# Keys first: another load and work order, running KV sums, and one kind of PSUM tile, in a gated mix of linear attention and an MLP

## The chip, the cores and the metric

The kernel runs on one core of a Trainium2 chip. The metric is the device time of a run in microseconds (us), the median of several runs. The "span" of a profile is shorter, because it goes from the core's first to its last instruction: for the kernel before, 165.8 us of span stand for about 167.5 us of time. Engines: PE is TensorE's matmuls, PEld its weight loads, DVE is VectorE, ACT is ScalarE, POOL is GpSimd, SP is SyncE, which here only issues transfers (SPq).

## The reference, cut to what matters

x is 2048 tokens by 448, in bf16. Branch A is linear attention with 16 heads of 28 and softmax features; branch B is an MLP with tanh gelu, 448 to 1792 and back. A gate g per token mixes them.

```python
q, k, v = split(x @ wqkv)                       # 16 heads of 28
phi_q = concat([softmax(q @ w_phi), softmax(-(q @ w_phi))])
phi_k = concat([softmax(k @ w_phi), softmax(-(k @ w_phi))])
kv, z = phi_k.T @ v, phi_k.sum(0)               # sums over all 2048 tokens
a = ((phi_q @ kv) / (phi_q @ z + 1e-6)) @ wo
b = gelu(x @ w1 + b1) @ w2 + b2
g = sigmoid((x * gate_w).sum(-1))
out = g * a + (1 - g) * b
```

The projection weights are folded with w_phi on the chip (Wpk for keys, Wpq for queries) before any key or query can be computed; keys need an exponential on ScalarE, then sums and reciprocals on VectorE, then a normalisation; all key tiles have to be summed into kv before the first "nm" tile (numerator and denominator); and PE does the rest.

## The kernel before: the parts that the change and the argument touch

The main order, with what each step is called in the profile in the comments:

```python
for t in range(4):
    v_tile(t, late=True)         # v: 4 matmuls of 448 columns into a one-bank PSUM tile
prep(WkT, Wpk)                   # w_ps: fold w_phi into the key weights, copies by DVE and ACT
prep_twice(WqT, Wpq)             # w_ps: the same for queries
k_pair(0)
k_pair(1)
late_logits(range(4))            # l_ps: the gate logits of the first four tiles
for u in range(2, 4):
    v_tile(2 * u); v_tile(2 * u + 1); k_pair(u)
b1_turn()                        # b1p: transpose the MLP's bias b1
for u in range(4, 8):
    v_tile(2 * u); v_tile(2 * u + 1); k_pair(u); q_pair(u - 4, 0)
q_pair(0, 1); q_pair(1, 1)
kv_group(0)                      # 32 matmuls of 116 columns over all key tiles
q_pair(2, 1); kv_group(1); q_pair(3, 1); kv_group(2); kv_group(3)
# [...]  gate, gelu table
for t in range(2): num_tile(t)   # nm, then a chain of 11 DVE instructions, then a transposing DMA to oT
for n in range(28): m_unit(n // 14, n % 14)      # hp: 14 row-paired matmuls, then gelu on ACT
for t in range(16):
    if t + 2 < 16: num_tile(t + 2)
    # y: 4 matmuls of oT with wo, 14 of gel with w2, then scaled on ACT (res) and stored
```

```python
def k_pair(u):
    pk = pair("pk")              # a two-bank PSUM tile
    # [...] 8 matmuls of 448 columns
    nc.scalar.activation(out=phik[:, tt, 0, :], in_=pk[:, :, 0:D], func=ACT.Exp)
    nc.scalar.activation(out=phik[:, tt, 1, :], in_=pk[:, :, 0:D], func=ACT.Exp, scale=-1.0)
    nc.vector.reduce_sum(out=sums[:], in_=ph, axis=AX.X)
    nc.vector.reciprocal(out=rec[:], in_=sums[:])
    eng = nc.vector if u >= 6 else nc.gpsimd
    eng.tensor_tensor(out=ph, in0=ph, in1=rec[...], op=ALU.mult)
```

PSUM has four one-bank tiles (v, w_ps, kv, nm) and two two-bank tiles (pk, pq, hp, y), so nm never takes a buffer from hp or y.

The softmax here doesn't subtract the row's maximum and nothing guards it: scores larger than these inputs give would overflow.

## Time and profile before

| | before |
|---|---|
| time | 167.38 us median (3 runs) |
| span | 165.8 us |
| PE busy | 159.1 us, 96% |
| PE's waits after the warm-up | 1.7 us in five places, the longest 0.5 |
| DVE, ACT busy | 84.3 and 79.6 us |
| clock granted to PE in every slice | 1.00 |

How to read it: an engine that is busy 96% of the span, and whose few waits are all short, sets the span. The lines that carry this reading are in the prediction below.

### The profile page before, as it was taken

To read this page: it belongs to the slowest core of one execution; us is meant where nothing else is said; L and a number is where in the kernel's file an instruction comes from. 1 tells how busy PE (TensorE), PEld (TensorE's weight loads), DVE (VectorE), ACT (ScalarE), POOL (GpSimd) and SP (SyncE) were. 2 spreads that over 40 slices of the span, in tenths; PEclk is the share of its full clock that TensorE was granted. 3 is DMA by queue.
4 is the path that set the end of the run, shared out by engine and by line. 5 is a ranking of instruction groups with operands and counts; after the bars stand their busy time and mean duration, and the time that the engine had idled before them with its cause. 6 is when DMAs were issued, how large, how long until landed. Compare 5 with 4: busy or idle time off the path is not lost.

```text
span 165.8 us, 3129 instructions
## 1 busy us (share of the span) xinstructions
PE 159.1 (96%) x1278; PEld 84.6 (51%) x1278; DVE 84.3 (51%) x250; ACT 79.6 (48%) x99; POOL 25.6 (15%) x36
## 2 busy tenths in 40 slices
PE   6899999999999999999999999999999999999991
PEld 2356544444366855444545445555555555555450
DVE  1255699975981286000000004887877777778300
ACT  2045877889884477777777775111112211111111
POOL 5810099996000000000000000000000000000000
PEclk9999999999999999999999999999999999999999
DMA  5999989999900001100000000222222253325300
GB/s 118 224 214 152 215 169 227 214 209 232 338 9 4 4 2 32 36 0 0 0 4 0 0 4 0 59 59 63 60 59 61 59 65 76 72 60 63 89 28 28
DMA packets 28348, 13.72 MB, mean 83 GB/s; under 512 B 21805, under 2 KB 27438, under 8 KB 28334
## 3 DMA queue, kind: packets, MB, share of 16 engines
q1 hardware_dynamic: 27310, 13.09, 37.5%
q10 hardware_dynamic: 960, 0.43, 1.2%
q8 instruction: 10, 0.16, 0.4%
q14 instruction: 4, 0.03, 0.1%
q0 software_dynamic: 64, 0.00, 0.0%
HBM read 5.65 MB, written 1.84 MB: 45 GB/s over the span
## 4 chain that ended last, share of the span: by engine, by line
PE 73%; SPq 10%; DMA 7%; DVE 6%; ACT 1%; issue 1%; DVEq 0%; ACTq 0%
PE hp L336 26%; PE y L394 24%; PE y L391 7%; PE nm L348 4%; PE pq L265 4%; PE kv L278 3%; PE v_ps L184 3%; SPq L115 3%; PE pk L247 3%; DMA xT<-in_A_x_dram 3%; SPq L116 3%; DMA oT<-o_tok 3%; SPq L119 3%; DVE phik L258 2%; DVE sums L254 2%; DMA b1c<-in_B_b_dram 1%
## 5 line engine op out<-in xcount | busy, mean ns | idle before, releaser
L394 PE MATMUL y<-w_sb,gel 128*128 128x448 bf16 x224 | 45.0, 352 | 0.0
L336 PE MATMUL hp<-xT,w_sb 64*128 64x512 bf16 x196 | 42.5, 376 | 0.0
L336 PE MATMUL hp<-xS,w_sb 64*128 64x512 bf16 x196 | 42.5, 376 | 0.0
L339 ACT ACTIVATE gel<-hp,b1T 128x1024 bf16<-128x1024 f32 x28 | 31.2, 1114 | 11.1 <-PE hp L336 10.6
L397 ACT ACTIVATE res<-y,ungate 128x448 bf16<-128x448 f32 x16 | 10.1, 634 | 50.5 <-PE y L394 50.5
L394 PEld LDWEIGHTS <-gel 128*128 128x128 bf16 x224 | 21.9, 98 | 20.5
L336 PEld LDWEIGHTS <-w_sb 64*128 64x128 bf16 x392 | 20.8, 94 | 21.3
L352 DVE COPY st<-nm 128x32 f32<-128x32 f32 x32 | 4.5, 183 | 44.6 <-PE nm L348 44.6
L258 POOL TENSOR_TENSOR phik<-phik,rec 128x1792 bf16<-128x1792 bf16 x6 | 19.1, 3209 | 12.3 <-DVE rec L256 12.3
L254 DVE TENSOR_REDUCE sums<-phik 128x64 f32<-128x1792 bf16 x8 | 16.1, 2007 | 5.5 <-ACT phik L251 5.5
L369 DVE TENSOR_TENSOR tmp<-nm,al 128x448 bf16<-128x448 f32 x32 | 18.4, 615 | 0.0
L391 PE MATMUL y<-wo_sb,oT 128*128 128x448 bf16 x64 | 14.8, 352 | 0.4 <-DMA oT<-o_tok 0.4
L184 PE MATMUL v_ps<-WvG,xT 128*128 128x449 bf16 (+1 forms) x64 | 13.7, 356 | 0.5 <-DMA xT<-in_A_x_dram 0.5
L265 PE MATMUL pq<-xT,Wpq 64*128 64x512 bf16 x56 | 13.5, 377 | 0.3 <-ACT phik L251 0.2
L265 PE MATMUL pq<-xS,Wpq 64*128 64x512 bf16 x56 | 13.4, 377 | 0.0
L247 PE MATMUL pk<-Wpk,xT 128*128 128x448 bf16 x64 | 13.2, 352 | 0.0
L250 ACT ACTIVATE phik<-pk 128x896 bf16<-128x896 f32 x8 | 7.3, 918 | 6.9 <-PE pk L247 6.9
L270 ACT ACTIVATE EqP<-pq 112x1024 bf16<-112x1024 f32 x8 | 8.2, 1024 | 3.2 <-PE pq L265 3.2
L184 PEld LDWEIGHTS <-xT 128*128 128x128 bf16 x64 | 5.8, 99 | 7.5 <-issue 1.5
L247 PEld LDWEIGHTS <-xT 128*128 128x128 bf16 x64 | 6.2, 98 | 5.8
L265 PEld LDWEIGHTS <-Wpq 64*128 64x128 bf16 x112 | 5.1, 94 | 7.4 <-issue 2.4
L348 PE MATMUL nm<-KVbd,EqP 112*128 112x120 bf16 x64 | 8.6, 216 | 0.0
(71 smaller groups left out, 138.0 us busy)
## 6 DMA issues: line engine op xcount, KB each, us to landing
w_sb<-in_B_w_dram SPq DMA_DIRECT2D x3, 1568.0 KB, 18.7
out_dram<-res SPq DMA_DIRECT2D x16, 112.0 KB, 1.9
xS<-xT SPq DMA_DIRECT2D x2, 256.0 KB, 3.8
xS<-xT SPq DMA_DIRECT2D x2, 192.0 KB, 3.6
WvG<-in_A_wqkv_dram ACTq DMA_DIRECT2D x1, 336.0 KB, 3.4
wo_sb<-in_A_wo_dram SPq DMA_DIRECT2D x1, 336.0 KB, 18.7
oT<-o_tok SPq DMA_TRANSPOSE x16, 2.4
xT<-in_A_x_dram SPq DMA_TRANSPOSE x8, 4.5
```

The source lines that it names most:

```text
L184: nc.tensor.matmul(v_ps[:, 0:n], lhsT=xT[:, c, t * P:(t + 1) * P], rhs=WvG[:, c, 0:n], start=(c == 0), stop=(c == NC4 - 1))
L247: nc.tensor.matmul(pk[:, i, 0:D], lhsT=xT[:, c, t * P:(t + 1) * P], rhs=Wpk[:, c, :], start=(c == 0), stop=(c == NC4 - 1))
L254: nc.vector.reduce_sum(out=sums[:], in_=ph, axis=AX.X)
L258: eng.tensor_tensor(out=ph, in0=ph, in1=rec[:, :, None].to_broadcast([P, 64, DH]), op=ALU.mult)
L265: nc.tensor.matmul(pq[:, i, :], lhsT=Wpq[i * HP:(i + 1) * HP, k, g * GW:g * GW + P], rhs=x_half(i, k, h), start=(k == 0), stop=(k == NK - 1))
L336: nc.tensor.matmul(hp[:, i, :], lhsT=w1_sb[i * HP:(i + 1) * HP, k, j * P:(j + 1) * P], rhs=x_half(i, k, h), start=(k == 0), stop=(k == NK ...
L339: nc.scalar.activation(out=gel[:, j, h * 1024:(h + 1) * 1024], in_=hp[:].rearrange("p a b -> p (a b)"), func=ACT.Gelu_apprx_tanh, bias=b1T ...
L348: nc.tensor.matmul(nm[s][:, g * KW:(g + 1) * KW], lhsT=E[0:GW, g, tok], rhs=KVbd[0:GW, g, s, :], start=True, stop=True)
L369: nc.vector.tensor_tensor(out=tmp[:, s, :].rearrange("p (g j d) -> p g j d", g=NG, j=4), in0=nm[s][:, 0:NG * KW].rearrange("p (g c) -> p g ...
L391: nc.tensor.matmul(y, lhsT=oT[:, c, tok], rhs=wo_sb[:, c, :], start=(c == 0), stop=False)
L394: nc.tensor.matmul(y, lhsT=gel[:, j, tok], rhs=w2_sb[:, j, :], start=False, stop=(j == NJ - 1))
L397: nc.scalar.activation(out=res[:], in_=y, func=ACT.Copy, scale=ungate[:, t:t + 1])
```

## The change

Its intent: load and compute the keys first, so that their exponentials, sums and normalisation are under way early; sum kv while keys are still coming, in two PSUM banks that stay open; save PE work by pairing the half-filled last chunk (448 = 3 x 128 + 64) of v with that of k on the two row halves of the array; use two-bank PSUM tiles alone, three of them beside the two open banks, so that v is copied out two tiles at a time; split the gelu buffer, so that the first half can be written while keys are still being summed.

The diff, cut to its core:

```diff
-    ps = ctx.enter_context(tc.tile_pool(name="ps", bufs=4, space=PSUM))   # "one" x4, "pair" x2
+    def pair(name):
+        return ps.tile([P, 2, 512], F32, name=name, tag="pair", bufs=3)
+    acc = ps.tile([P, 2, 512], F32, name="acc", tag="acc", bufs=1)
-    load_x(0); load_wT(WkT, D); load_wT(WqT, 0); load_x(1); load_x(2) [...]
+    load_wT(WkT, D); load_x(0); load_x(1); load_wT(WqT, 0); swap_x(0) [... v weights, load_x(2), ...]
     # order of the work
-    v_tile(0..3); prep(WkT, Wpk); prep_twice(WqT, Wpq); k_pair(0); k_pair(1); late_logits(range(4))
-    [...]
+    dummies(10)
+    prep(WkT, Wpk)
+    dummies(3)
+    for u in range(4):
+        k_pair(u)
+    prep_twice(WqT, Wpq)
+    for u in range(4):
+        q_pair(u, 0)
+        v_pair(u)
+    b1_turn()
+    kv_pair(4); q_pair(0, 1); kv_sum(0); kv_sum(1)
+    kv_pair(5); q_pair(1, 1); kv_sum(2); kv_sum(3)
+    kv_pair(6); q_pair(2, 1); kv_sum(4); kv_pair(7); q_pair(3, 1); kv_sum(5)
     # prep_twice: copies two chunks at a time, on DVE for m = 0 and 2, on ACT for m = 1 and 3
+            copy(m + 1, W_out[:, 2 * m:2 * m + n, 0:D], w_ps[:, 0:n, 0:D])
+    def kv_pair(u):                       # v and k of two token tiles
+        [... c = 0..2 of v, then of k, for both tiles ...]
+        for i in range(2):
+            nc.tensor.matmul(v_ps[:, i, 0:D + 1], lhsT=x3, rhs=WvL[:], start=False, stop=True)
+            nc.tensor.matmul(pk[:, i, 0:D], lhsT=xT[HP:P, 3, ...], rhs=Wpk[HP:P, 3, :], ...)
+        k_out(u, pk)                      # exponentials, sums, reciprocal, normalisation
+        v_out(u, v_ps)                    # copies on DVE
     # hp and y
-    AHEAD = 2
+    AHEAD = 3
+        if n == 2: kv_sum(6); kv_sum(7); kv_out()
+        if n == 4: num_tile(0); num_tile(1)
+    num_tile(2)
```

More of the change, by code (lines that the diff above doesn't have):

```diff
@@ L55 @@
     work = ctx.enter_context(tc.tile_pool(name="work", bufs=2))
-    ps = ctx.enter_context(tc.tile_pool(name="ps", bufs=4, space=PSUM))
-    def one(name):
-        return ps.tile([P, 512], F32, name=name, tag="one", bufs=4)
+    ps = ctx.enter_context(tc.tile_pool(name="ps", bufs=3, space=PSUM))
     def pair(name):
-        return ps.tile([P, 2, 512], F32, name=name, tag="pair", bufs=2)
+        return ps.tile([P, 2, 512], F32, name=name, tag="pair", bufs=3)
     xT = consts.tile([P, NC4, S], BF16, name="xT")
     xS = consts.tile([P, NC4, 2, 512], BF16, name="xS")
+    x3o = consts.tile([HP, 512], BF16, name="x3o")
     w1_sb = consts.tile([P, NK, F], BF16, name="w1_sb")
@@ L82 @@
     ungate = consts.tile([P, NT], F32, name="ungate")
+    hold = ctx.enter_context(tc.tile_pool(name="hold", bufs=1))
+    phik_all = hold.tile([P, NT * 2 * D + 16], BF16, name="phik", tag="phik_gel")
+    phik = phik_all[:, 0:NT * 2 * D].rearrange("p (t s f) -> p t s f", t=NT, s=2)
+    vaug = hold.tile([P, NT, NG, GW + 4], BF16, name="vaug")
     atn = ExitStack()
@@ L86 @@
     WvG = attn.tile([P, NC4, D + 1], BF16, name="WvG")
+    WvL = attn.tile([HP, D + 1], BF16, name="WvL")
     Wpk = attn.tile([P, NC4, D], BF16, name="Wpk")
@@ L93 @@
     bd = attn.tile([P, NC4, H, DH], BF16, name="bd")
-    phik_all = attn.tile([P, NT * 2 * D + 16], BF16, name="phik")
-    phik = phik_all[:, 0:NT * 2 * D].rearrange("p (t s f) -> p t s f", t=NT, s=2)
-    vaug = attn.tile([P, NT, NG, GW + 4], BF16, name="vaug")
     warm = attn.tile([P, 512], BF16, name="warm")
     nc.vector.memset(warm[:], 0.0)
+    nc.vector.memset(wphi[64:P, 3, :], 0.0)
     nc.vector.memset(WvG[0:64, 3, :], 0.0)
-    nc.vector.memset(wphi[64:P, 3, :], 0.0)
-    nc.scalar.dma_start(WvG[:, 0:3, 0:D],
-                        A_wqkv[0:384, 2 * D:3 * D].rearrange("(c p) n -> p c n", p=P))
-    nc.scalar.dma_start(WvG[64:P, 3, 0:D], A_wqkv[384:448, 2 * D:3 * D])
     wphi_rows = A_w_phi.rearrange("h a b -> (h a) b")
@@ L111 @@
     nc.gpsimd.dma_start(WvG[64:P, 3, D:D + 1], gate_w[384:448, None])
+    nc.gpsimd.dma_start(WvL[:, D:D + 1], gate_w[384:448, None])
     def load_x(b):
@@ L119, in load_wT, with swap_x @@
         nc.sync.dma_start_transpose(W[:], A_wqkv[:, base:base + NC4 * P])
-    load_x(0)
-    load_wT(WkT, D)
-    load_wT(WqT, 0)
-    load_x(1)
-    load_x(2)
-    for h in range(2):
-        if h == 1:
-            load_x(3)
+    def swap_x(h):
         ev = slice(2 * h * 512, 2 * h * 512 + 512)
@@ L132 @@
         nc.sync.dma_start(xS[HP:P, 0:3, h, :], xT[0:HP, 0:3, od])
+    load_wT(WkT, D)
+    load_x(0)
+    load_x(1)
+    load_wT(WqT, 0)
+    swap_x(0)
+    nc.sync.dma_start(WvG[:, 0:3, 0:D],
+                      A_wqkv[0:384, 2 * D:3 * D].rearrange("(c p) n -> p c n", p=P))
+    nc.sync.dma_start(WvG[64:P, 3, 0:D], A_wqkv[384:448, 2 * D:3 * D])
+    nc.sync.dma_start(WvL[:, 0:D], A_wqkv[384:448, 2 * D:3 * D])
+    load_x(2)
+    load_x(3)
+    swap_x(1)
+    nc.sync.dma_start(x3o[:], xT[HP:P, 3, 1536:2048])
     nc.sync.dma_start(b1c[:], B_b1.rearrange("(j p) -> j p", p=P))
@@ L177 @@
     nc.gpsimd.memset(o_tok[:, :, D + 1:512], 0.0)
-    def v_tile(t, late=False):
-        v_ps = one("v_ps")
-        n = D if late else D + 1
-        for c in range(NC4):
-            nc.tensor.matmul(v_ps[:, 0:n], lhsT=xT[:, c, t * P:(t + 1) * P],
-                             rhs=WvG[:, c, 0:n], start=(c == 0), stop=(c == NC4 - 1))
-        src = v_ps[:, 0:D].rearrange("p (g d) -> p g d", g=NG)
-        if t % 2 == 0:
-            nc.scalar.copy(out=vaug[:, t, :, 0:GW], in_=src)
-            if not late:
-                nc.scalar.copy(out=lg[:, t:t + 1], in_=v_ps[:, D:D + 1])
-        else:
-            nc.vector.tensor_copy(out=vaug[:, t, :, 0:GW], in_=src)
-            if not late:
-                nc.vector.tensor_copy(out=lg[:, t:t + 1], in_=v_ps[:, D:D + 1])
@@ L196, in late_logits @@
-    def late_logits(tiles):
-        l_ps = one("l_ps")
-        for t in tiles:
-            for c in range(NC4):
-                nc.tensor.matmul(l_ps[:, t:t + 1], lhsT=xT[:, c, t * P:(t + 1) * P],
-                                 rhs=WvG[:, c, D:D + 1], start=(c == 0), stop=(c == NC4 - 1))
-        nc.vector.tensor_copy(out=lg[:, tiles[0]:tiles[-1] + 1],
-                              in_=l_ps[:, tiles[0]:tiles[-1] + 1])
-    def prep(W_T, W_out):
-        for c in range(NC4):
-            dlo = c * P if c < 3 else 320
-            w_ps = one("w_ps")
-            for e, (h0, h1) in enumerate(spans):
-                nc.tensor.matmul(w_ps[:, h0 * DH:h1 * DH], lhsT=W_T[:, e, dlo:dlo + P],
-                                 rhs=bd[:, e, h0:h1, :].rearrange("p h d -> p (h d)"),
-                                 start=(e == 0), stop=(e == NC4 - 1), skip_group_check=True)
-            lo = 0 if c < 3 else 64
-            if c % 2 == 0:
-                nc.vector.tensor_copy(out=W_out[lo:P, c, 0:D], in_=w_ps[lo:P, 0:D])
-            else:
-                nc.scalar.copy(out=W_out[lo:P, c, 0:D], in_=w_ps[lo:P, 0:D])
@@ L219, in prep_twice, with v_out @@
-    def prep_twice(W_T, W_out):
-        for k in range(NK):
-            w_ps = one("w_ps")
-            for e, (h0, h1) in enumerate(spans):
-                for i in range(2):
-                    nc.tensor.matmul(w_ps[i * HP:(i + 1) * HP, h0 * DH:h1 * DH],
-                                     lhsT=W_T[:, e, k * HP:(k + 1) * HP],
+    def v_out(u, v_ps):
+        tt = slice(2 * u, 2 * u + 2)
+        nc.vector.tensor_copy(out=vaug[:, tt, :, 0:GW],
+                              in_=v_ps[:, :, 0:D].rearrange("p i (g d) -> p i g d", g=NG))
+        nc.vector.tensor_copy(out=lg[:, tt], in_=v_ps[:, :, D])
@@ new lines, in v_pair, with copy @@
+    def v_pair(u):
+        v_ps = pair("v_ps")
+        for i in range(2):
+            t = 2 * u + i
+            for c in range(NC4):
+                nc.tensor.matmul(v_ps[:, i, 0:D + 1], lhsT=xT[:, c, t * P:(t + 1) * P],
+                                 rhs=WvG[:, c, :], start=(c == 0), stop=(c == NC4 - 1))
+        v_out(u, v_ps)
+    def copy(k, out, in_):
+        if k % 2 == 0:
+            nc.scalar.copy(out=out, in_=in_)
+        else:
+            nc.vector.tensor_copy(out=out, in_=in_)
@@ L226, in prep_twice @@
+    def prep(W_T, W_out):
+        for m in range(2):
+            w_ps = pair("w_ps")
+            for i in range(2):
+                c = 2 * m + i
+                dlo = c * P if c < 3 else 320
+                for e, (h0, h1) in enumerate(spans):
+                    nc.tensor.matmul(w_ps[:, i, h0 * DH:h1 * DH], lhsT=W_T[:, e, dlo:dlo + P],
                                      rhs=bd[:, e, h0:h1, :].rearrange("p h d -> p (h d)"),
                                      start=(e == 0), stop=(e == NC4 - 1), skip_group_check=True)
-            if k % 2 == 0:
-                nc.vector.tensor_copy(out=W_out[:, k, 0:D], in_=w_ps[:, 0:D])
-            else:
-                nc.scalar.copy(out=W_out[:, k, 0:D], in_=w_ps[:, 0:D])
+            if m == 0:
+                copy(0, W_out[:, 0, :], w_ps[:, 0, 0:D])
+                copy(1, W_out[:, 1, :], w_ps[:, 1, 0:D])
+            else:
+                copy(0, W_out[:, 2, :], w_ps[:, 0, 0:D])
+                copy(1, W_out[64:P, 3, :], w_ps[64:P, 1, 0:D])
@@ new lines, in prep_twice @@
+    def prep_twice(W_T, W_out):
+        for m in range(4):
+            w_ps = pair("w_ps")
+            n = 2 if m < 3 else 1
+            for ii in range(n):
+                k = 2 * m + ii
+                for e, (h0, h1) in enumerate(spans):
+                    for i in range(2):
+                        nc.tensor.matmul(w_ps[i * HP:(i + 1) * HP, ii, h0 * DH:h1 * DH],
+                                         lhsT=W_T[:, e, k * HP:(k + 1) * HP],
+                                         rhs=bd[:, e, h0:h1, :].rearrange("p h d -> p (h d)"),
+                                         start=(e == 0), stop=(e == NC4 - 1),
+                                         skip_group_check=True)
+            copy(m + 1, W_out[:, 2 * m:2 * m + n, 0:D], w_ps[:, 0:n, 0:D])
@@ L240, in x_half, with k_out @@
         return xS[rows, k // 2, h, :]
-    def k_pair(u):
-        pk = pair("pk")
-        for i in range(2):
-            t = 2 * u + i
-            for c in range(NC4):
-                nc.tensor.matmul(pk[:, i, 0:D], lhsT=xT[:, c, t * P:(t + 1) * P],
-                                 rhs=Wpk[:, c, :], start=(c == 0), stop=(c == NC4 - 1))
+    def k_out(u, pk):
         tt = slice(2 * u, 2 * u + 2)
@@ L256, in k_pair @@
         nc.vector.reciprocal(out=rec[:], in_=sums[:])
-        eng = nc.vector if u >= 6 else nc.gpsimd
-        eng.tensor_tensor(out=ph, in0=ph,
-                          in1=rec[:, :, None].to_broadcast([P, 64, DH]), op=ALU.mult)
+        parts = [(nc.gpsimd, 0, 64)] if u < 7 else [(nc.vector, 0, 32), (nc.gpsimd, 32, 64)]
+        for eng, lo, hi in parts:
+            eng.tensor_tensor(out=ph[:, lo:hi], in0=ph[:, lo:hi],
+                              in1=rec[:, lo:hi, None].to_broadcast([P, hi - lo, DH]), op=ALU.mult)
+    def k_pair(u):
+        pk = pair("pk")
+        for i in range(2):
+            t = 2 * u + i
+            for c in range(NC4):
+                nc.tensor.matmul(pk[:, i, 0:D], lhsT=xT[:, c, t * P:(t + 1) * P],
+                                 rhs=Wpk[:, c, :], start=(c == 0), stop=(c == NC4 - 1))
+        k_out(u, pk)
+    def kv_pair(u):
+        v_ps = pair("v_ps")
+        pk = pair("pk")
+        for i in range(2):
+            t = 2 * u + i
+            for c in range(3):
+                nc.tensor.matmul(v_ps[:, i, 0:D + 1], lhsT=xT[:, c, t * P:(t + 1) * P],
+                                 rhs=WvG[:, c, :], start=(c == 0), stop=False)
+            for c in range(3):
+                nc.tensor.matmul(pk[:, i, 0:D], lhsT=xT[:, c, t * P:(t + 1) * P],
+                                 rhs=Wpk[:, c, :], start=(c == 0), stop=False)
+        for i in range(2):
+            t = 2 * u + i
+            off = (t % 4) * P
+            x3 = x3o[:, off:off + P] if t >= 12 else xS[0:HP, 3, 1, off:off + P]
+            nc.tensor.matmul(v_ps[:, i, 0:D + 1], lhsT=x3, rhs=WvL[:], start=False, stop=True)
+            nc.tensor.matmul(pk[:, i, 0:D], lhsT=xT[HP:P, 3, t * P:(t + 1) * P],
+                             rhs=Wpk[HP:P, 3, :], start=False, stop=True)
+        k_out(u, pk)
+        v_out(u, v_ps)
     def q_pair(g, h):
@@ L271, in q_pair, with kv_sum @@
         nc.scalar.activation(out=EqN[0:GW, g, dst], in_=src, func=ACT.Exp, scale=-1.0)
-    def kv_group(g):
-        kv = [one("kv"), one("kv")]
-        for t in range(NT):
-            for s in range(2):
-                lo = (t * 2 + s) * D + g * GW
-                nc.tensor.matmul(kv[s][:, 0:GW + 4], lhsT=phik_all[:, lo:lo + P],
-                                 rhs=vaug[:, t, g, :], start=(t == 0), stop=(t == NT - 1))
+    acc = ps.tile([P, 2, 512], F32, name="acc", tag="acc", bufs=1)
+    def kv_sum(u):
+        for t in (2 * u, 2 * u + 1):
+            for g in range(NG):
+                for s in range(2):
+                    lo = (t * 2 + s) * D + g * GW
+                    nc.tensor.matmul(acc[:, s, g * (GW + 4):(g + 1) * (GW + 4)],
+                                     lhsT=phik_all[:, lo:lo + P], rhs=vaug[:, t, g, :],
+                                     start=(t == 0 and g == 0), stop=(t == NT - 1),
+                                     skip_group_check=True)
@@ L280, in kv_group, with kv_out @@
+    def kv_out():
         for s in range(2):
-            nc.vector.tensor_tensor(out=KVbd[0:GW, g, s, 0:GW + 4], in0=kv[s][0:GW, 0:GW + 4],
-                                    in1=mask[0:GW, :], op=ALU.mult)
+            nc.vector.tensor_tensor(
+                out=KVbd[0:GW, :, s, 0:GW + 4],
+                in0=acc[0:GW, s, 0:NG * (GW + 4)].rearrange("p (g c) -> p g c", g=NG),
+                in1=mask[0:GW, None, :].to_broadcast([GW, NG, GW + 4]), op=ALU.mult)
     def b1_turn():
-        tp = ps.tile([P, 16], BF16, name="b1p", tag="one", bufs=4)
+        tp = ps.tile([P, 16], BF16, name="b1p", tag="pair", bufs=3)
@@ L286, in b1_turn, with dummies @@
         nc.tensor.transpose(tp[:, 0:NJ], b1c[:], ident[:])
         nc.vector.tensor_copy(out=b1T[:], in_=tp[:, 0:NJ])
-    w_ps = one("warm_ps")
-    for _ in range(13):
-        nc.tensor.matmul(w_ps[:], lhsT=warm[:, 0:P], rhs=warm[:], start=True, stop=True)
-    for t in range(4):
-        v_tile(t, late=True)
+    def dummies(n):
+        w_ps = pair("warm_ps")
+        for _ in range(n):
+            nc.tensor.matmul(w_ps[:, 0, :], lhsT=warm[:, 0:P], rhs=warm[:], start=True, stop=True)
+    dummies(10)
@@ L295 @@
     prep(WkT, Wpk)
+    dummies(3)
+    for u in range(4):
+        k_pair(u)
     prep_twice(WqT, Wpq)
-    k_pair(0)
-    k_pair(1)
-    late_logits(range(4))
-    for u in range(2, 4):
-        v_tile(2 * u)
-        v_tile(2 * u + 1)
-        k_pair(u)
-    b1_turn()
-    for u in range(4, 8):
-        v_tile(2 * u)
-        v_tile(2 * u + 1)
-        k_pair(u)
-        q_pair(u - 4, 0)
+    for u in range(4):
+        q_pair(u, 0)
+        v_pair(u)
+    b1_turn()
+    kv_pair(4)
     q_pair(0, 1)
+    kv_sum(0)
@@ L313 @@
+    kv_sum(1)
+    kv_pair(5)
     q_pair(1, 1)
-    kv_group(0)
+    kv_sum(2)
+    kv_sum(3)
+    kv_pair(6)
     q_pair(2, 1)
-    kv_group(1)
+    kv_sum(4)
+    kv_pair(7)
     q_pair(3, 1)
-    kv_group(2)
-    kv_group(3)
+    kv_sum(5)
     nc.vector.tensor_scalar(out=lg[:], in0=lg[:], scalar1=60.0, scalar2=None, op0=ALU.min)
@@ L327 @@
     atn.close()
-    late = ctx.enter_context(tc.tile_pool(name="late", bufs=1))
-    gel = late.tile([P, NJ, S], BF16, name="gel")
+    late = ctx.enter_context(tc.tile_pool(name="late", bufs=1, reuse_waits="tile"))
+    gel = [late.tile([P, NJ, S // 2], BF16, name="gel0"), None]
     def m_unit(h, j):
@@ L338, in m_unit @@
                                  rhs=x_half(i, k, h), start=(k == 0), stop=(k == NK - 1))
-        nc.scalar.activation(out=gel[:, j, h * 1024:(h + 1) * 1024],
+        if gel[h] is None:
+            gel[h] = hold.tile([P, NJ, S // 2], BF16, name="gel1", tag="phik_gel")
+        nc.scalar.activation(out=gel[h][:, j, :],
                              in_=hp[:].rearrange("p a b -> p (a b)"),
@@ L344, in num_tile @@
         tok = slice(t * P, (t + 1) * P)
-        nm = [one("nm"), one("nm")]
+        nm_ps = pair("nm")
+        nm = [nm_ps[:, 0, :], nm_ps[:, 1, :]]
         for g in range(NG):
@@ L376, in num_tile @@
         nc.sync.dma_start_transpose(oT[:, :, tok], o_tok[:, t % 4, :])
-    AHEAD = 2
-    for t in range(AHEAD):
-        num_tile(t)
+    AHEAD = 3
     for n in range(2 * NJ):
         m_unit(n // NJ, n % NJ)
+        if n == 2:
+            kv_sum(6)
+            kv_sum(7)
+            kv_out()
+        if n == 4:
+            num_tile(0)
+            num_tile(1)
+    num_tile(2)
     for t in range(NT):
@@ L393 @@
         for j in range(NJ):
-            nc.tensor.matmul(y, lhsT=gel[:, j, tok], rhs=w2_sb[:, j, :],
+            nc.tensor.matmul(y, lhsT=gel[t // 8][:, j, (t % 8) * P:(t % 8 + 1) * P], rhs=w2_sb[:, j, :],
                              start=False, stop=(j == NJ - 1))
```

## The prediction

> **What bounds the kernel now.** I read the busy shares first, then the waits of the matmul engine, then the chain that ended last. The page's first part and the waits of PE:
>
> ```profile
> PE 159.1 (96%) x1278; PEld 84.6 (51%) x1278; DVE 84.3 (51%) x250; ACT 79.6 (48%) x99; POOL 25.6 (15%) x36
> ```
> ```profile
> PE warm_ps L292 <- DVE warm L100: 1.3, 1, 1.3
> PE v_ps L184 <- DMA xT<-in_A_x_dram: 0.5, 1, 0.5
> PE y L391 <- DMA oT<-o_tok: 0.4, 1, 0.4
> PE w_ps L210 <- ACT Wpk L217: 0.4, 1, 0.4
> PE pq L265 <- ACT phik L251: 0.2, 1, 0.2
> PE kv L278 <- DVE phik L258: 0.2, 1, 0.2
> ```
> PE is the bound: its first useful matmul starts at 6.78 us, and from there to its last it waits 1.7 us in all. So a change can win only by removing PE work, by starting earlier, or by collecting that 1.7 us. It can lose without limit: PE has no slack, so every new PE wait is added to the span. The prices of PE work come from the chain in order of time (start, length, what):
> ```profile
> 24.41 1.64 PE v_ps L184 x8
> 26.05 1.51 PE pk L247 x8
> 27.57 1.62 PE pq L265 x14
> 50.94 1.73 PE kv L278 x32
> 58.78 42.41 PE hp L336 x392
> 101.72 0.76 PE y L391 x4
> 102.48 2.65 PE y L394 x14
> 105.13 0.42 PE nm L348 x8
> ```
> Read: a 128-row matmul of 448 columns costs 1.51/8 = 0.189 us; a 64-row one of 512 columns 1.62/14 = 0.116, because two run side by side; 32 kv products 1.73; one hp unit 42.41/28 = 1.515; one y tile 3.41; one nm tile 0.42.
>
> [...]the logits copy below is ready when PE ends at 18.0, yet DVE runs it at 22.91, behind the k sums and reciprocals put before it:
> ```profile
> 17.47 0.54 PE L200 MATMUL l_ps<-WvG,xT 128*128 128x1 bf16 x16
> 17.92 2.02 DVE L254 TENSOR_REDUCE sums<-phik 128x64 f32<-128x1792 bf16 x1 [2.75 <-ACT phik L251]
> 20.44 1.96 DVE L254 TENSOR_REDUCE sums<-phik 128x64 f32<-128x1792 bf16 x1
> 22.44 0.55 DVE L256 RECIPROCAL rec<-sums 128x64 f32<-128x64 f32 x1
> 22.91 0.10 DVE L202 COPY lg<-l_ps 128x4 f32<-128x4 f32 x1
> ```
> [...]The trace's 13 warm-up matmuls of 512 columns take 5.73 us, 0.43 apart or 0.83 ns a column, where a 448-column one later takes 0.189/448 = 0.42 ns; a later fall back to the slow rate is in no run here.
>
> **The change, part by part.**
> Removed from PE: the late logits (16 matmuls, 17.47 to 17.88: 0.4). In the paired v and k, 8 matmuls of each of four pairs become 6+6 full ones and two pairs of half-row ones: 14 slots for 16, so 4 x 2 x 0.189 = 1.5[...]. Also perhaps the oT wait (0.4). Gains: about 2 us.
>
> Moved: WkT is the first transpose on SyncE's queue, x after it. Before, the first two x transposes (issued 0.81 and 2.24) took 5.6 and 5.8 us to land and WkT (4.18) 5.3, that is 6.4, 8.05 and 9.5. The queue takes them 1.4 to 2.3 us apart, so now WkT lands near 6.5, the two halves of x block 0 near 8.2 and 9.6. The k weights allow nothing sooner: bd ends near 6.9 (wphi lands about 0.81+4.8, then four products, 1.2), 12 more products, then four Wpk copies of about 0.55, each DVE one made to wait for ACT's: near 9.1. So k pair 0 passes its last chunk at 9.6 and ends at 9.6+5x0.189 = 10.6; the two exponentials (second one 0.8 after the first, 0.9 long) end at 12.4.
>
> Here is the trap. The built order of DVE is: four times (sums, reciprocal), and only then the two double-width copies of Wpq. One sums plus reciprocal costs 17.92 to 20.44 = 2.52. So the first Wpq copy starts at 12.4+4x2.52 = 22.5. Price of a copy from L229, twice its width (448 more elements add about 0.47 to 0.625): 1.1. They end at 23.6 and 24.7. PE in the meantime ends k pair 3 near 15.1, does three quarters of the Wpq products as buffers return (last near 18.4), and stands still until 23.6, as q pair 0 is next in its queue and needs that copy. Idle: about 5 us, after some 1.5 us in pieces.
>
> From 23.6 PE still has: 8 q x 1.62 = 13.0; 4 v x 1.56 = 6.2; 4 paired v,k x (14x0.189+0.15) = 11.2; kv sums 4x1.73 = 6.9; nm 16x0.42 = 6.7; hp 42.4; y 16x3.41 = 54.6. Sum 141.0. After the last matmul the old kernel needs 165.8-162.3 = 3.5. So 23.6+141.0+3.5 = 168.1, plus 0.5, by which the same sum falls short on the old kernel from its 24.34 on: **168.6 with no further wait**, already 2.8 over the old 165.8.
>
> Added waits: with three pair buffers for everything (two for sums), each buffer returns through an ACT or DVE reader. I followed the buffer each tile gets in the built program.
> - q pair 0, half way, for the second Wpq copy: 0.3.
> - first paired v,k: v takes the buffer of q pair 3 (exponentials 1.94 after its end, PE spends 1.6 on v): 0.35; k that of the last v, copied by DVE in 1.25: 0.33.
> - last paired k behind the exponentials of q: 0.5.
> - hp unit 2 takes the buffer of the last v, whose copy now stands on DVE behind sums, reciprocal and half a normalisation (2.52+1.0+1.3 after the exponentials): 0.85.
> - nm 0 and 1 now take hp buffers for as long as DVE works on them (101.70 to 104.50 before: 2.8): hp 5, 6, 8 wait 0.35+0.7+0.2 = 1.25.
> - y 0 behind the last gelu 0.4, y 1 behind y 0's scaling 0.4, y 2 behind nm 4, DVE having three nm tiles of 3.2 queued: 0.5.
> Sum 4.9. Span 168.6+4.9 = 173.5. Two more items: [...]overlaps I took too pessimistically, perhaps 1.5. I leave the span at 173. The timed runs exceed the profile's span by 167.38-165.8 = 1.6: **174.6 us**.
>
> **Rivals.**
> (1) The intent holds: kv sums hidden in the exponentials, no waits, row pairing pays 1.5, time near 165. For it: PE work falls by 2 us, and the old kernel's ACT and DVE are half idle. Against: it needs the Wpq copies before 19, and FIFO order forbids it.
> (2) The gap exists but is refilled: time 169 to 170.5. It is so if x lands a microsecond earlier (first exponential from 11.3) and the buffer waits overlap; for it, the ACT weight load no longer shares the DMA engines in the first 4 us. Against: the Wpk copies bind at 9.1 anyway, so at most 0.6 comes back.
> (3) DMA becomes the bound: x blocks 2 and 3 and the swaps now come after more loads. SyncE issues them about 1.5 apart, so they land near 25; they are wanted from 36. Hidden; w1 later still, wanted at 61. I give it little.
> [...]
>
> **Range and chances.** No-wait floor 168.6+1.6 = 170.2; within 2% means at most 170.7, so nearly every buffer wait would have to vanish or the start be a microsecond faster: 0.12. Faster by over 2% (below 164.0) would need the DVE queue to be wrong: 0.02. The rest 0.86. Range 171.0 to 178.0: the low end is half of the added waits gone[...].
>
> **What would show it.** In the changed profile: PE idle before the pq matmuls near 18 to 24, ended by the DVE copy of Wpq; DVE without a break from about 12.4 to 24.7; q pair 0 near 23.6; hp's first unit near 61 (58.7 before); PE waits at hp ended by ACT and DVE; no wait for oT; warm durations after the gap or not (matmul spacing 0.38 against 0.19 in the first v pair). The prediction is wrong if the sums are shorter, if Wpq's copies come before them, or if PE's order lets other work fill the gap.

The gains of "about 2 us" were 0.4 + 1.5 + 0.4, less 0.4 that is cut. The span was 168.6 + 4.9 = 173.5, plus 1.2 for a term that is cut (a fall of the clock after the gap), less 1.5 for the overlaps: 173.2, left at 173, and 174.6 with the 1.6. The cut term at its worst also made the upper end of the range, 178, and it alone made a fourth rival. Two allowances are estimates, with no source given: 0.47 us for 448 more elements of a copy (measured: 1.10 for 896 in the changed kernel, 0.625 for 448 before, so 0.47), and 0.15 a paired tile (measured: 2.76 us, 45.10 to 47.86 in the changed kernel's chain, 0.11 over 14 x 0.189). "FIFO order" is what the logits copy shows: ready at 18.0, run at 22.91, behind what was put before it.

## The result, and the profile after

The changed kernel takes **177.68 us** (177.36 to 178.43, 4 runs) against 167.56 us (167.18 to 167.76, 4 runs) of the kernel before in the same rounds. The ratio is 1.0613, with a 95% interval of 1.0573 to 1.0654. Here and below a ratio is the mean time of one kernel's fast runs over that of the other's of the same rounds, so it is not quite the ratio of the medians.

The span went from 165.8 to 175.6 us. The busy line of the page, after (to compare with 159.1 before):

```profile
PE 159.9 (91%) x1262; PEld 83.5 (48%) x1262; DVE 84.9 (48%) x242; ACT 74.7 (43%) x84; POOL 31.5 (18%) x39
```

PE is busy for almost as long as before (why not for less is taken up further below), but it stands still for 175.6 - 159.9 = 15.7 us instead of 165.8 - 159.1 = 6.7. So 9.0 of the 9.8 us are idle time. PE's six longest waits in the changed kernel (who waited, for whom, us, times, longest):

```profile
PE pq L296 <- DVE Wpq L205: 5.2, 1, 5.2
PE warm_ps L331 <- DVE warm L101: 1.3, 1, 1.3
PE hp L376 <- DVE lg L190: 1.2, 1, 1.2
PE w_ps L232 <- ACT phik L251: 1.0, 1, 1.0
PE pk L280 <- ACT EqN L302: 0.7, 1, 0.7
PE hp L376 <- DVE tmp L412: 0.5, 1, 0.5
```

One wait of 5.2 us, for a copy by VectorE, is more than half of the loss. All waits but this and the warm-up's add up to 5.6 us, where the kernel before had 1.7: 3.9 more. And 5.15 + 3.9 is the 9.0. The wait for the transposed oT is gone, as foretold. What VectorE did before that copy is in its timeline (start, length, engine, line, operation):

```profile
12.03 2.02 DVE L254 TENSOR_REDUCE sums<-phik 128x64 f32<-128x1792 bf16 x1 [3.12 <-ACT phik L251]
14.09 0.55 DVE L256 RECIPROCAL rec<-sums 128x64 f32<-128x64 f32 x1
...
19.49 1.96 DVE L254 TENSOR_REDUCE sums<-phik 128x64 f32<-128x1792 bf16 x1
21.55 0.55 DVE L256 RECIPROCAL rec<-sums 128x64 f32<-128x64 f32 x1
22.14 2.09 DVE L205 CAST Wpq<-w_ps 128x896 bf16<-128x896 f32 x2
```

From 12.03 to 24.23 it never rests for more than 0.1 us: four times sums and reciprocal, one unit every 2.5 us, then the copy. The matmuls whose result it copies began at 14.71 us, so that result lay ready for some 7 us.

A last part of the loss is inside the busy time. The stretch view, after, one microsecond a row, with the rows from 21 to 26 left out (busy time of PE, PEld, DVE, ACT and POOL, then the granted clock, the DMA share and GB/s):

```profile
19.00:20.00 1.00, 0.00 (x0) 0.00 (x0) 0.98 (x2) 0.00 (x0) 1.00 (x1) 1.00 0.25 10
20.00:21.00 1.00, 0.00 (x0) 0.00 (x0) 1.00 (x1) 0.00 (x0) 1.00 (x1) 0.65 1.06 198
26.00:27.00 1.00, 1.00 (x6) 0.28 (x3) 0.00 (x0) 0.51 (x1) 1.00 (x1) 0.50 0.54 65
27.00:28.00 1.00, 1.00 (x6) 0.50 (x5) 0.00 (x0) 1.00 (x2) 0.52 (x1) 0.94 0.81 222
```

The clock falls to one half inside the idle stretch, at about 20.3, which is 2.2 us after PE's last matmul (it ends at 18.13), and comes back at about 27.1: from shares of 0.65 and 0.94 the edges are 20 + 0.3 and 27 + 0.12. PE works again from 23.28, so the first query and value pairs are multiplied at half speed: the query matmuls start 0.43 us apart, for 0.22 in the next pair. All four runs show it (mean granted clock 0.976 to 0.981, against 1.000 in the profile before).

### The profile page after: what moved, and what is told of

It is laid out like the page before. It is cut to its first block, busy times and chain, and to the rows that moved or that the text cites. A ratio compares the mean times of both kernels' runs of the same rounds, so it can differ in the third digit from the quotient of the medians.

```text
span 175.6 us, 3100 instructions
## 1 busy us (share of the span) xinstructions
PE 159.9 (91%) x1262; PEld 83.5 (48%) x1262; DVE 84.9 (48%) x242; ACT 74.7 (43%) x84; POOL 31.5 (18%) x39
## 4 chain that ended last, share of the span: by engine, by line
PE 72%; DVE 16%; ACT 4%; DMA 4%; issue 1%; SPq 1%; DVEq 0%; ACTq 0%
PE hp L376 22%; PE y L443 21%; PE pq L296 6%; PE y L440 6%; DVE sums L254 6%; PE v_ps L197 4%; DMA xT<-in_A_x_dram 4%; PE nm L391 3%; PE acc L311 3%; PE pk L280 3%; DVE tmp L412 2%; PE v_ps L277 2%; DVE rec L256 2%; ACT phik L250 2%; ACT phik L251 1%; DVE vaug L188 1%
## 5 line engine op out<-in xcount | busy, mean ns | idle before, releaser
L376 PE MATMUL hp<-xT,w_sb 64*128 64x512 bf16 x196 | 43.3, 376 | 2.0 <-DVE lg L190 1.2
L376 PE MATMUL hp<-xS,w_sb 64*128 64x512 bf16 x196 | 43.2, 376 | 0.0
L446 ACT ACTIVATE res<-y,ungate 128x448 bf16<-128x448 f32 x16 | 10.1, 634 | 51.2 <-PE y L443 51.2
L259 POOL TENSOR_TENSOR phik<-phik,rec 128x1792 bf16<-128x1792 bf16 (+1 forms) x8 | 24.9, 3126 | 33.1 <-DVE rec L256 33.1
L296 PE MATMUL pq<-xT,Wpq 64*128 64x512 bf16 x56 | 14.9, 408 | 5.2 <-DVE Wpq L205 5.2
L296 PE MATMUL pq<-xS,Wpq 64*128 64x512 bf16 x56 | 14.9, 408 | 0.0
L188 DVE CAST vaug<-v_ps 128x896 bf16<-128x896 f32 x8 | 8.5, 1067 | 10.6 <-PE v_ps L197 10.6
L391 PE MATMUL nm<-KVbd,EqN 112*128 112x120 bf16 x64 | 8.2, 215 | 0.0
L302 ACT ACTIVATE EqN<-pq 112x1024 bf16<-112x1024 f32 x8 | 8.2, 1027 | 0.0
L440 PEld LDWEIGHTS <-oT 128*128 128x128 bf16 x64 | 5.7, 97 | 4.7 <-issue 1.2
```

Of the source, the lines that this page charges most:

```text
L188: nc.vector.tensor_copy(out=vaug[:, tt, :, 0:GW], in_=v_ps[:, :, 0:D].rearrange("p i (g d) -> p i g d", g=NG))
L259: eng.tensor_tensor(out=ph[:, lo:hi], in0=ph[:, lo:hi], in1=rec[:, lo:hi, None].to_broadcast([P, hi - lo, DH]), op=ALU.mult)
L296: nc.tensor.matmul(pq[:, i, :], lhsT=Wpq[i * HP:(i + 1) * HP, k, g * GW:g * GW + P], rhs=x_half(i, k, h), start=(k == 0), stop=(k == NK - 1))
L376: nc.tensor.matmul(hp[:, i, :], lhsT=w1_sb[i * HP:(i + 1) * HP, k, j * P:(j + 1) * P], rhs=x_half(i, k, h), start=(k == 0), stop=(k == NK ...
L391: nc.tensor.matmul(nm[s][:, g * KW:(g + 1) * KW], lhsT=E[0:GW, g, tok], rhs=KVbd[0:GW, g, s, :], start=True, stop=True)
L440: nc.tensor.matmul(y, lhsT=oT[:, c, tok], rhs=wo_sb[:, c, :], start=(c == 0), stop=False)
```

## The experiments

Ten kernels, all correct against the reference. Spans are of their profiles; a ratio is always against the kernel before in the same rounds.

### 1. The Wpq copies ahead of two of the sums

The theory to test is that VectorE's queue order makes the 5 us. The rival is that the start is bound by landings or exponentials, so that another wait would take its place. Only the order of VectorE's (and with it GpSimd's) instructions changes:

```diff
     for u in range(4):
-        k_pair(u)
+        k_pair(u, norm=(u < 2))      # exponentials at once; sums of pairs 2, 3 later
     prep_twice(WqT, Wpq)
     for u in range(4):
         q_pair(u, 0)
         v_pair(u)
+        if u in (1, 2):
+            k_norm(u + 1)
```

> The changed kernel with the sums and reciprocals of k pairs 2 and 3 moved on VectorE behind the Wpq copies (after v pairs 1 and 2); same instructions otherwise. Queue theory: the first Wpq copy starts near 17.1 instead of 22.1, q pair 0 at 18.2 instead of 23.3, the 5.15 us wait and the half clock both vanish, span 175.6 - 5.1 - 1.9 = about 168.6, granted clock 1.000. Rival (the start is bound by DMA landings or the exponentials, the copy is only the last of several waits): another wait of several us takes its place at pq and the span stays above 173.

Measured: 171.42 us, ratio 1.0267 (1.0234 to 1.0301), span 169.6, granted clock 0.997 (0.996 to 1.000 in the four runs, as in the seven of the kernel before in these rounds). VectorE's timeline in this kernel:

```profile
16.65 0.55 DVE L259 RECIPROCAL rec<-sums 128x64 f32<-128x64 f32 x1
17.23 2.09 DVE L205 CAST Wpq<-w_ps 128x896 bf16<-128x896 f32 x2
```
```profile
PE pq L305 <- DVE Wpq L205: 0.2, 1, 0.2
```

The copy starts 4.9 us earlier and the wait falls from 5.2 to 0.2 us; the slow clock is gone with it (the first query and value pairs, 18.38 to 21.84, take 3.46 us instead of 5.16). The span falls by 6.0 us, not by the 7.0 that I expected: a wait of the first paired k for the copy of the last v, which VectorE now does behind a sum, is 0.7 us here. The theory stands and the rival falls.

### 2. The same gap, filled with dummy work

```diff
     prep_twice(WqT, Wpq)
+    for _ in range(22):
+        nc.tensor.matmul(acc[:, 0, :], lhsT=warm[:, 0:P], rhs=warm[:], start=True, stop=True)
```

The products go to a bank that the kv sums clear later, so no buffer is taken from anyone.

> The changed kernel with 22 dummy matmuls (22 x 0.216 = 4.75 us) into the sums' bank in the gap before q pair 0, nothing else. Cooling theory: the gap's length stays (q pair 0 still near 23.3), but q pair 0 and v pair 0 run at full clock, so the span falls by 1.9 us to 173.7, granted clock 1.000. Rival (the slow first q and v are due to the second Wpq copy or to late xS): span stays at 175.6 within 0.4.

Measured: 176.07 us, ratio 1.0536 (1.0508 to 1.0565), span 174.5, granted clock 1.000. The chain in order of time, first of the changed kernel, then of this one:

```profile
23.28 3.17 PE pq L296 x14
26.45 1.99 PE v_ps L197 x8
```
```profile
23.82 1.82 PE pq L296 x14
25.64 1.64 PE v_ps L197 x8
```

The gap is as long as before (the x block landed 0.5 us later in this run, 9.09 against 8.55, and all that follows is shifted). But the first query and value pairs take 3.46 us instead of 5.16. So the slow clock costs **1.7 us**, separate from the gap. Useless work made the kernel faster by 0.7% (1.0536 against 1.0613).

### 3. The pairing undone

```diff
-            for c in range(3): [v]     for c in range(3): [k]
-        [the two half-row pairs]
+            for c in range(4): [v]     for c in range(4): [k]
```

> The changed kernel with the last chunk of v and k unpaired again for pairs 4 to 7 (16 full matmuls instead of 12 and 2 pairs). Price list theory: 4 x 2 x 0.189 = 1.5 us more PE work[...], span about 176.7 (1.1 more). Rival (the paired stretch is bound by the exponentials and sums, not by PE): same within 0.3.

(The 1.1 was the 1.5 less a term of 0.4.)

Measured: 178.58 us, ratio 1.0699 (1.0663 to 1.0735), span 177.0. In the chain, values, keys and the queries after them take from 45.77 to 50.43 = 4.66 us unpaired, and 45.10 to 49.38 = 4.28 us paired. The difference, 0.38, is two matmuls of 0.189. Nothing behind the paired chunk is slower for it: the queries that follow are row-paired themselves and take 1.51 us after a paired chunk, 1.62 after a full one. The chain, first of the changed kernel, then of this one:

```profile
47.86 1.51 PE pq L296 x14
```
```profile
48.81 1.62 PE pq L289 x14
```

So the pairing is worth 4 x 0.38 = 1.5 us of PE time. Undoing it costs 1.4 us by the spans and by the ratios (the medians, 0.9 apart, are of different rounds). The 1.4 are the 1.5 us of matmuls, less 0.6 because the waits of pk and hp behind them are shorter here (0.3 and 1.0, for 0.7 and 1.2), plus 0.3 because the slow clock costs more in this run (the first query and value pairs take 5.43 us, for 5.16), plus 0.2 because PE passes the first x block later (8.75 for 8.55).

### 4. The pairing alone, in the kernel before

The function kv_pair from the change, with one-bank v tiles, and its two small loads; everything else as before.

```diff
     for u in range(4, 8):
-        v_tile(2 * u)
-        v_tile(2 * u + 1)
-        k_pair(u)
+        kv_pair(u)
         q_pair(u - 4, 0)
```

> The kernel before with that one part of the change added: row-paired last chunk of v and k for pairs 4 to 7 (with the two small loads it needs), PSUM and load order as before. If the pairing is worth its PE time: 1.1 to 1.5 us less than before, span about 164.5. Rival: ScalarE, which then holds 0.73 + 1.6 + 1.9 us of work per 4.4 us, or late landings give it back: within 0.4 of before or slower.

Measured: 167.13 us, ratio 1.0008 (0.9975 to 1.0041): no gain. PE's busy time fell from 159.1 to 156.5 us, but its waits show where that went:

```profile
PE b1p L320 <- DMA b1c<-in_B_b_dram: 0.9, 1, 0.9
PE pq L299 <- ACT phik L285: 0.6, 1, 0.6
PE kv L312 <- DVE phik L292: 0.5, 1, 0.5
```

The two new loads delay the small bias load (issued at 23.09 us, for 21.91 before), for which PE waits; and further on PE reaches the end of the keys sooner than their exponentials and normalisation do. (PE also waits 1.0 us longer for the x blocks in this run, 1.5 for 0.5, but that cost nothing: the 13 warm-up matmuls took 4.43 us instead of 5.73, and PE goes on at 7.99, for 8.07 before. This is also why PE's busy time fell by more than the pairing's 1.5.) The b1p wait of 0.9, with 0.4 more for pq and 0.3 more for kv, makes up for the pairing's 1.5. A gain on the bound engine is only a gain if those that serve it keep up.

### 5. Values copied out ahead of the sums

On top of the first experiment, for pairs 4 to 7:

```diff
-        k_out(u, pk)
-        v_out(u, v_ps)
+        k_exp(u, pk)
+        v_out(u, v_ps)
+        k_norm(u)
```

> The first experiment (copies first, span 169.6) with one more edit: for pairs 4 to 7 VectorE copies v out before it sums k, not after. Buffer theory: hp's third unit no longer waits 1.2 us for the buffer of the last v, span about 168.4. Rival (the wait only hides another, the exponential's end or the first gelu): another PE wait of about 1 us appears there and the span stays within 0.3 of 169.6.

Measured: 170.64 us, ratio 1.0195 (1.0165 to 1.0226), span 169.1. That is 0.7% better than the first experiment by the ratios, 0.3% by the spans. The wait of hp for the copied v did vanish, but the rival is half right, as the first gelu takes its place:

```profile
PE hp L388 <- ACT gel L393: 1.0, 2, 0.7
```

### 6. The nm tiles apart from one another

On top of the first experiment:

```diff
-        if n == 4:
-            num_tile(0); num_tile(1)
-    num_tile(2)
+        if n in (6, 11, 16, 21):
+            num_tile((n - 6) // 5)
-    AHEAD = 3
+    AHEAD = 4
```

> The first experiment with one more edit: four nm tiles spread over the hp units (after units 6, 11, 16, 21), none in a row, four ahead of y. Buffer theory: the waits of hp for nm's buffers (0.5 + 0.3) and of y for gel, res and tmp (0.3 + 0.3 + 0.3) go, span about 168.0. Rival (three pair buffers are too few anyhow): the waits move to other units, span within 0.4 of 169.6.

Measured: 169.72 us, ratio 1.0144 (1.0111 to 1.0177), span 168.0. All five waits of hp and y for nm, gelu and res buffers (0.5 + 0.3 + 0.3 + 0.3 + 0.3 = 1.7) are gone from the list, and the span is 1.6 us shorter. So with two-bank tiles shared among nm, hp and y, the nm tiles in a row cost 1.7 us here, and spread out they cost none that the list shows. The edit also puts a fourth nm tile ahead of y; what that alone is worth, for the three waits of y above all, was not run.

### 7. The waits mended, in the changed kernel

Experiments 5 and 6 together, and the Wpq copies behind the first sums already, the first Wpq product in the sums' bank, and one kv sum moved forward to before kv_pair(4), and one put off until just before kv_pair(7).

```diff
-            w_ps = pair("w_ps")
+            w_ps = acc if m == 0 else pair("w_ps")
-        k_pair(u)
+        k_pair(u, norm=(u < 1))      # and k_norm(u + 1) after each v_pair(u), u < 3
+    kv_sum(0)
     kv_pair(4); q_pair(0, 1)
-    kv_sum(0)
     kv_sum(1)
     kv_pair(5); q_pair(1, 1); kv_sum(2)
-    kv_sum(3)
     kv_pair(6); q_pair(2, 1)
+    kv_sum(3)
     kv_sum(4)
```

> Both edits together, and: Wpq copies already behind the first sums, first Wpq products in the sums' bank, one kv sum moved ahead of the first paired v and k and one ahead of the last. If the change loses only by its waits, all of them are gone but the 1 us at the start: span 164.5 to 165, just under the kernel before (165.8). If keys first costs something else: over 166.5.

Measured: 167.57 us, ratio 1.0011 (0.9980 to 1.0041), span 165.9. That is 10 us better than the change as it came, and level with the kernel before; my expectation was 1 us too low. What is left, beside five waits of 0.4 to 0.8 us near the start and at the first paired keys, is

```profile
PE hp L388 <- ACT gel L393: 1.2, 1, 1.2
```

So the last sums now stand in front of PE less, but the first gelu, which ACT can begin only after the last exponentials, the gate and a table load (1.28 us in both kernels' traces), stands there more. This last cause is read from the list; I have not taken it away.

### 8. The pairing in the kernel before, with its waits mended

Experiment 4, with b1_turn moved behind the first queries of the second half, the small loads reordered, the exponentials of a pair ahead of its v copies on ScalarE, the normalisation of pair 6 given to GpSimd and that of pair 7 split between VectorE and GpSimd, one q_pair ahead of kv_group(0), and three nm tiles ahead of y.

```diff
-    b1_turn()
     [... second half of the keys ...]
-    kv_group(0); q_pair(2, 1); kv_group(1); q_pair(3, 1)
+    b1_turn(); q_pair(2, 1); kv_group(0); q_pair(3, 1); kv_group(1)
     # the normalisation
-    eng = nc.vector if u >= 6 else nc.gpsimd
+    parts = [(nc.gpsimd, 0, 64)] if u < 7 else [(nc.vector, 0, 40), (nc.gpsimd, 40, 64)]
-    AHEAD = 2
+    AHEAD = 3                        # the third nm tile after hp's unit 8
```

> The fourth experiment (kernel before with paired chunks, no gain) with what stood in the way moved: b1 turned later, exponentials ahead of the v copies on ScalarE, last normalisation split with GpSimd, a q pair ahead of the first kv group, three nm tiles ahead of y. If the pairing's 1.5 us were lost to three waits (b1c 0.9, pq 0.6, kv 0.5): span 163.5 to 164.2, ratio near 0.99. If ScalarE is the bound of that stretch: within 0.4 us of the kernel before.

Measured: **165.87 us**, ratio 0.9908 (0.9879 to 0.9937), span 164.2. Of the waits of experiment 4, b1p's and kv's are gone. It beats both kernels, the one before by 0.9%. Six things were moved at once, and the same moves without the pairing were not run. One of them, the third nm tile, also took away a wait that the kernel before has without any pairing (0.4 us of y for oT). So the gain of 1.6 us of span is about the pairing's 1.5, but it is not shown that the pairing alone makes it, nor what each move is worth.

### 9. Half the dose of experiment 1

Only the sum of pair 3 goes behind the copies.

```diff
-        k_pair(u, norm=(u < 2))
+        k_pair(u, norm=(u < 3))
-        if u in (1, 2):
+        if u == 2:
             k_norm(u + 1)
```

> The changed kernel with the sums and reciprocal of k pair 3 alone moved behind the Wpq copies (half the dose of the first experiment). Queue theory: one unit of 2.5 us leaves the queue ahead of the copy, the wait of pq falls from 5.15 to about 2.65 us. Cooling theory: [...]1.7 us more go than the queue alone explains, span 175.6 - 2.5 - 1.7 = 171.4. Rival (the cooling comes with any gap): q and v 0 still slow, span 173.

Measured: 175.78 us, ratio 1.0509 (1.0468 to 1.0549), span 173.7. The queue theory is exact: the wait of pq is 2.6 us.

```profile
PE pq L305 <- DVE Wpq L205: 2.6, 1, 2.6
```

My expectation of the clock was wrong. The first query and value pairs (21.05 to 26.14) take 5.09 us, 1.63 more than at full clock (3.46, experiments 1 and 2), although PE never stood still for longer than 2.6 us (the row from 24 to 25 is left out):

```profile
21.00:22.00 1.00, 0.95 (x8) 0.31 (x8) 0.99 (x1) 0.00 (x0) 1.00 (x2) 1.00 1.21 250
22.00:23.00 1.00, 1.00 (x8) 0.27 (x6) 0.00 (x0) 0.00 (x0) 1.00 (x1) 0.59 0.91 171
23.00:24.00 1.00, 1.00 (x4) 0.27 (x3) 0.00 (x0) 0.55 (x1) 1.00 (x1) 0.50 0.76 158
25.00:26.00 1.00, 1.00 (x5) 0.27 (x2) 0.00 (x0) 0.39 (x1) 0.00 (x0) 0.70 0.86 201
```

The clock falls at about 22.2, more than a microsecond after PE has begun to work again (at 21.05), and it returns at about 25.6. So here it fell while PE was working (busy 0.95 and 1.00 of the rows from 21 and 22). What sets the moment is not shown; the last section puts the runs side by side.

### 10. Values of tiles 12 and 14 copied by VectorE

On top of experiment 8:

```diff
-        if t % 2 == 0:
+        if t % 2 == 0 and t < 12:
             nc.scalar.copy(out=vaug[:, t, :, 0:GW], in_=src)
```

> The best kernel so far (kernel before, mended, 164.2) with the v copies of tiles 12 and 14 on VectorE. If ScalarE's queue causes the 0.9 us that pq still waits: 0.5 to 0.9 less, span 163.5. Rival (VectorE becomes the late one, through the sums of pair 7): no gain or a wait of kv instead.

Measured: **165.53 us**, ratio 0.9891 (0.9858 to 0.9923), span 164.1. One of the two pq waits (0.6) is gone from the list, but the span is only 0.1 shorter, and the interval overlaps that of experiment 8; a gain over it is not shown. It is the fastest kernel, 1.1% under the kernel before.

The runs in one table:

| kernel | median us | ratio to before | span us |
|---|---|---|---|
| before (rounds of the change) | 167.56 | 1 | 165.8 |
| changed | 177.68 | 1.0613 | 175.6 |
| 3: pairing undone | 178.58 | 1.0699 | 177.0 |
| 9: one sum behind the copies | 175.78 | 1.0509 | 173.7 |
| 2: gap filled with dummies | 176.07 | 1.0536 | 174.5 |
| 1: two sums behind the copies | 171.42 | 1.0267 | 169.6 |
| 5: 1, and values ahead of the sums | 170.64 | 1.0195 | 169.1 |
| 6: 1, and nm tiles apart | 169.72 | 1.0144 | 168.0 |
| 7: the waits mended | 167.57 | 1.0011 | 165.9 |
| 4: before, paired | 167.13 | 1.0008 | 165.5 |
| 8: before, paired and mended | 165.87 | 0.9908 | 164.2 |
| 10: 8, and two v copies on VectorE | 165.53 | 0.9891 | 164.1 |

## Why the prediction was right, and where it was off

It forecast 174.6 us, slower by over 2% with a chance of 0.86, and a range of 171 to 178. Measured were 177.68, just inside the upper end: of a loss of 10.1 us it had foretold 7.2. The cause was right, the sum was too low. Point by point:

- **PE is the bound and has no slack.** Right: 9.0 of the 9.8 us added to the span are PE's idle time, although PE has less work.
- **The trap in VectorE's queue.** Right, and shown by experiments 1 and 9: two units of sums moved, the wait falls from 5.2 to 0.2; one unit, to 2.6. First copy foretold at 22.5, measured at 22.14; first query pair foretold at 23.6, measured at 23.28; gap foretold at about 5, measured 5.15. Both times are some 0.3 early: PE passed x block 0 at 8.55 in this run (it began the first keys then, and ended them at 10.25, not 10.6). hp's first unit, foretold near 61, began at 62.3.
- **The slow clock.** This term, at even odds and so 1.2 us in the sum, is cut from the prediction. That there could be a fall was right, the odds were too low: the granted clock was 0.50 for 6.8 us in the profiled run, and all four runs have a mean of 0.976 to 0.981; it costs 1.7 us (experiment 2). Experiment 9 shows that even half the gap brings it about.
- **The added buffer waits, 4.9 us.** Right in kind: every place named but one shows a wait in the trace (the first queries did not wait for the second Wpq copy, foretold as 0.3). The sizes for hp's third unit were 1.2 for 0.85; for hp behind nm 0.8 for 1.25; for y 0.8 for 1.3; for the last paired k 0.7 for 0.5. Experiment 6 shows those of hp and y behind nm, gelu and res to be worth 1.6 us. The list has eight waits after the first query pair, 3.9 us in all. But a matmul of 448 columns is recorded as 0.352 us long while the next one can start 0.189 after it, so by an estimate each stop costs 0.16 more than its listed wait: 5.2 in all.
- **"Overlaps I took too pessimistically, perhaps 1.5."** This is the step that failed. I took 1.5 us off the sum without a row that says so. What came back is the 0.3 of the earlier start, and by the estimate above nothing of the waits. Without the 1.5, and without the clock's 1.2, the sum was 173.5; with the measured 1.7 of the slow clock it makes 175.2, and the profile says 175.6. In the prices, v pairs stand at 1.56 where the prediction's own line says 1.64, and queries behind a paired chunk at 1.62 where 1.51 was measured; the two about cancel. The last step was wrong as well: 167.38 - 165.8 = 1.6 takes the span of one run from the time of another. Run by run, time exceeds span by 1.7 to 1.8 us in both kernels (167.57 and 165.8; 177.36 and 175.6). The rest of the miss is that the profiled run is the fastest of the four, 0.3 under their median.
- **The gains, about 2 us.** The pairing's 1.5 is measured (experiment 3). The 0.4 taken off it was not found: the stretch compared there is 0.38 us longer unpaired, the whole of two full matmuls, and the queries behind a paired chunk are the shorter ones (1.51 us for 1.62).
- **Rivals.** The first (no waits) fell. The second (the gap is refilled) fell: the gap is there in full. The third (DMA) fell: the only landing that PE waits for is x's at the start, 0.4 us. The fourth (the clock falls after the gap) came true, with the 0.50 above.

What stays open: PE's busy time rose by 0.8 us. I can name 1.7 for the slow clock, less 1.5 for the pairing, 0.4 for the late logits and 0.5 for the warm-up matmuls (5.26 for 5.73); so 1.5 us of busy time is not accounted for by these. By the estimate above, the seven stops more than before (12 for 5, without the warm-up's) would add 7 x 0.16 = 1.1 of it; no run shows it. And which of the six moves in experiment 8 matter was not taken apart.

## What to carry to other kernels

Before moving a stage earlier, write down the order in which each helper engine will see its instructions, since a queue that serves in order turns "earlier for the keys" into "later for everything emitted after them"; here four sums of 2.5 us stood in front of a 1.1 us copy on which the bound engine waited. A part that saves work on the bound engine (the pairing, 1.5 us) can be worth nothing until the waits behind it are moved too: in the kernel before it gave nothing (experiment 4), while in the changed kernel it paid at once (experiment 3). When you have added up a sum from rows, do not take a round figure off it for luck, and take time and span from the same run.

## What the traces show of the clock

- Two falls, two runs without one. In the changed kernel, where PE waits 5.2 us for Wpq, the granted clock fell to 0.50 at about 20.3, 2.2 us after the last matmul, and was back at about 27.1, 6.8 us later. In experiment 9, where the wait is 2.6 us, it fell at about 22.2, 1.1 us after work had begun again, and was back at about 25.6, 3.4 us later. In experiment 1 the wait is 0.2 us, and in experiment 2 the gap is filled with matmuls: in both the first query and value pairs take 3.46 us, where the two others take 5.16 and 5.09. What sets the moment and the length of a fall is not shown; no run varied it on its own.
- A slow start that the row of the granted clock does not show. The 13 warm-up matmuls take 5.73 us in the kernel before, 0.43 apart, 0.83 ns a column for 0.42 later; yet the row says 1.00 there (every microsecond from 0 to 11). It did show the two falls above. So the matmul times have to be read beside it.
